# Where gT and w_out_r lie in SBUF: padded weight rows and three activation buffers at different byte offsets

## The chip, the core and the metric

The kernel runs on one core of a Trainium2 chip. A core has TensorE (matmuls, with a separate weight load before each), VectorE (DVE), ScalarE (ACT), GpSimd (POOL) and SyncE (SP, which only issues transfers here). Each engine takes its instructions strictly in order, and semaphores tie the engines to each other and to DMA transfers. Engines work on SBUF, whose tiles have 128 partitions and a byte address within the partition; matmuls write PSUM. The metric is the device time of one execution in microseconds; the median of several executions is compared.

## The reference

The input x has 8 sequences of 3008 positions with 256 channels. The first half is a spectral layer: a real FFT along the sequence, a complex 256x256 linear map with a bias, a soft threshold on real and imaginary parts, and the inverse FFT. The second half is a feed-forward layer on all 24064 positions: 256 to 2048, an ELU, and 2048 back to 256.

```python
X = np.fft.rfft(x, axis=1)
Yr = Xr @ w_r - Xi @ w_i + b_r          # and Yi alike
Yr = np.sign(Yr) * np.maximum(np.abs(Yr) - 0.01, 0.0)
y = np.fft.irfft(Yr + 1j * Yi, n=3008, axis=1)
h = y @ w_in
g = np.where(h > 0.0, h, np.exp(np.minimum(h, 0.0)) - 1.0)
out = g @ w_out                          # float32, 24064 x 256
```

## The kernel before

**The spectral layer.** 3008 = 47 x 64, and the FFT is done as matmuls in stages called units: A (`unit_A`, L129), X, M (the linear map), B and Y. Between A and X, and between B and Y, the data goes through DRAM, to come back with other rows on the partitions: A tiles are written to a DRAM tile DA (L157) and read back as Z (`load_Z`, L159); B tiles go to DB and come back as Bs (`load_Bs`, L267). Unit Y writes yT, the layer's output with channels on partitions, in bf16.

**The feed-forward layer.** The 24064 positions are cut into 47 blocks of 512, the 2048 hidden features into 8 pairs of 128-wide strips. One iteration i of the main loop (L844) is one block and one pair, so there are 376 iterations, 47 to a sequence. In an iteration:

- `front` (L705) computes hps, the hidden values of 2 strips for 512 positions, with four bf16 matmuls of 512 columns (L715). ACT then computes Et from it: exp (L729, or L724 in halves), or a relu and an exp (L726, L727).
- `elu` (L746) has DVE (L754) or POOL (L752) clamp Et.
- `finish_elu` (L734), called in the next iteration, has DVE combine hps and Et into gT (L740 or L742): 128 partitions by 2 strips by 512 positions in float32r, 4096 bytes per partition. This is also what frees hps in PSUM, of which there are two buffers in ordinary iterations, so `front` of two iterations later waits for it.
- `back` (L757), two iterations later (LAG = 2), multiplies gT by w_out_r: eight matmuls L773, each with a 128x128 slice of gT as weights and one 256-column row of w_out_r as the moving operand, both float32r, adding up in PSUM over the eight pairs. After the last pair the sums are copied to osb and sent to the output.

The units of the next sequences are spread over the iterations of the current one by `plan` (L800); each iteration carries at most a few of them ahead of its L715, in TensorE's order. The order of every engine is thus written out by the program; nothing is rearranged at run time.

**The tiles.** w_out_r (L64) is one SBUF tile of 16 rows of 256 float32r values per partition: row ft starts 1024 x ft bytes after the tile's start, and the tile's start is a multiple of 64 bytes. It is filled by two transfers from POOL's queue (`load_w_out`, L581). gT has a pool tag of its own with three buffers in `late3` (L566, L736), which lie 4096 bytes apart, all starting at a multiple of 64 bytes. The same three buffers serve once more: in the opening, unit A of the second sequence runs ahead (L663), and its second and third chunk (L133) take two of them, buffers 0 and 2 by address, until L157's transfers to DRAM have read them. In the built program the first gT of the main loop takes the remaining buffer, the second gT takes that same buffer again, and from the third on the buffers rotate. A gT that reuses a buffer waits for what read it last: an L773 group, or a transfer of A.

Of the kernel before, what the change touches and what calls it, by code (L numbers as in the profile page):

```python
# [10 lines left out]
BF16 = mybir.dt.bfloat16  # L11
F32 = mybir.dt.float32
F32R = mybir.dt.float32r
# [16 lines left out]
def kernel(  # L30
# [12 lines left out]
    P = nc.NUM_PARTITIONS  # L43

    B, S, D = x.shape
    assert D == 256 and S == N1 * N2
    DFF = moe_w_in.shape[1]
    E = moe_w_out.shape[1]
    assert E == 256 and DFF % (2 * P) == 0
    NFT = DFF // P  # L50
# [5 lines left out]
    constp = ctx.enter_context(tc.tile_pool(name="constp", bufs=1))  # L56
# [4 lines left out]
    wcat_r = constp.tile([P, 2, 2 * D], BF16, name="wcat_r")  # L61
    wcat_s = constp.tile([P, 2, 2 * D], BF16, name="wcat_s")
    w_in_s = constp.tile([P, 2, DFF], BF16, name="w_in_s")
    w_out_r = constp.tile([P, NFT, E], F32R, name="w_out_r")  # L64
    bias_bc = constp.tile([P, 2 * D], F32, name="bias_bc")
    bias_p = constp.tile([P, 2 * D], BF16, name="bias_p")
    lam_n = constp.tile([P, 1], F32, name="lam_n")
# [22 lines left out]
    TB = 512  # L90
# [4 lines left out]
    n = B * PER  # L95
# [3 lines left out]
    A_of = {}  # L99
# [18 lines left out]
    def unit_ps(name, alone):  # L118
        if alone:
            return pre2.tile([P, 2, 512], F32, name=name, tag="pre2")  # L120
        return psF.tile([P, 2, 512], F32, name=name, tag="fps")

    def evac(dst, src, on_dve):
        if on_dve:
            nc.vector.tensor_copy(dst, src)  # L125
        else:
            nc.scalar.copy(dst, src)  # L127

    def unit_A(b, u, alone=False, on_dve=False, ahead=False):  # L129
        ci, uu = u // 2, u % 2  # L130
        if uu == 0:
            if ahead and ci > 0:
                A_of[b, ci] = late3.tile([P, 8, D], BF16, name="A", tag="gT")  # L133
            elif alone:
                A_of[b, ci] = wk4.tile([P, 8, D], BF16, name="A", tag="Bs")
            else:
                A_of[b, ci] = wk2.tile([P, 8, D], BF16, name="A", tag="A")
            if ci == 0:
                DA_of[b] = dram.tile([NJ, P, D], BF16, name="DA", tag="DA")
        xt, A = xts[ci], A_of[b, ci]  # L140
        dav = DA_of[b].rearrange("j p d -> p j d")
        ps = unit_ps("aps", alone or ahead)
        for j in range(2):
            nc.tensor.matmul(  # L144
                ps[:, j, :], lhsT=M1[:],
                rhs=xt[:, 4 * uu + 2 * j : 4 * uu + 2 * j + 2, :], start=True, stop=True,
            )
        evac(
            A[:, 4 * uu : 4 * uu + 4, :].rearrange("p n d -> p (n d)"),
            ps[:].rearrange("p a b -> p (a b)"), on_dve,  # L150
        )
        j0 = 8 * ci
        if alone:
            j0 += 4 * uu
            nc.sync.dma_start(dav[:, j0 : j0 + 4, :], A[:, 4 * uu : 4 * uu + 4, :])
        elif uu == 1:
            nc.sync.dma_start(dav[:, j0 : j0 + 8, :], A[:])  # L157
# [155 lines left out]
    with tc.tile_pool(name="stagep", bufs=1) as stagep:  # L313
# [186 lines left out]
        def fA(u):  # L500
            unit_A(0, u, alone=True)
            if u < 5:
                idle_pe(3)
# [60 lines left out]
    gatep = ctx.enter_context(tc.tile_pool(name="gatep", bufs=2))  # L564
    late2 = ctx.enter_context(tc.tile_pool(name="late2", bufs=2))
    late3 = ctx.enter_context(tc.tile_pool(name="late3", bufs=3))  # L566

    w_in_v = moe_w_in.rearrange("(c p) f -> p c f", p=P)
    w_out_v = moe_w_out.rearrange("(t p) e -> p t e", p=P).bitcast(F32R)
# [93 lines left out]
    for u in range(6):  # L663
        unit_A(1, u, on_dve=bool(u % 2), ahead=True)
        if u == 1:
            scale_w_in(1, True)
            for w in (2, 3):
                load_Bs(0, w)
            gate(Bs_of[0, 2][:, 0, 0:1])
            load_w_out(1)  # L670
            load_w_in(3)
        idle_pe(2)
# [60 lines left out]

    def finish_elu():  # L734
        for i, hps, Et, whole, halves in late_elu:
            gT = late3.tile([P, 2, TB], F32R, name="gT", tag="gT")  # L736
            for s in range(2) if halves else (slice(0, 2),):
                o, h, e = gT[:, s], hps[:, s], Et[:, s]
                if whole:
                    nc.vector.scalar_tensor_tensor(o, e, -1.0, h, ALU.add, ALU.max)  # L740
                else:
                    nc.vector.scalar_tensor_tensor(o, h, 0.0, e, ALU.max, ALU.add)  # L742
            g_of[i] = gT
        late_elu.clear()
# [52 lines left out]
    def put(kind, b, *a):  # L797
        return ({"A": unit_A, "X": unit_X, "M": unit_M, "B": unit_B, "Y": unit_Y}[kind], (b, *a))
# [45 lines left out]
    for i in range(n + LAG):  # L844
        if i < n:
            r = i % PER
            if r == 0:
                f0, f1 = plan(i // PER)
                used = [bool(u0 or u1) for u0, u1 in zip(f0, f1)]
            free = not used[r]  # L850
            bare = bare + 1 if free else 0
            calm = free and (i >= n - 2 or (r + 2 < PER and not used[r + 1] and not used[r + 2]))
            for f, a in f0[r]:
                f(*a)
            on_act = any(f is unit_M for f, a in f0[r])
            h = front(i, calm and bare % 3 == 1, on_act, free and i > 0)
        finish_elu()
        if i < n:
            for f, a in f1[r]:
                f(*a)  # L860
            split = i > LAG and (i - LAG) % NPAIR == NPAIR - 1
            if split:
                back(i - LAG, True)
            elu(i, *h, free and i > 0, on_act)
        else:
            split = False
        if i >= LAG and not split:
            back(i - LAG, False)
# [30 lines left out]
```

## Time and profile before

| what | value |
|---|---|
| median of 3 executions | 911.94 us (911.36 to 913.53) |
| profiled execution | 911.36 us, of which span 909.6 us |
| granted TensorE clock, mean | 0.997 |
| L773, 3008 matmuls | busy 477.0 us |
| L715, 1728 matmuls | busy 389.9 us |
| DVE's gT (L740, L742), 470 instructions | 222.8 and 242.2 us |
| ACT's exp L729, 198 instructions | busy 204.0 us |

The profile's page gives busy times and shares for each engine; PE is TensorE's matmuls and PEld its weight loads, which overlap them. Matmuls are pipelined, and the end of one is modelled, so durations of neighbours overlap: what a matmul costs in a stream is the distance from its start to the next start. The chain of work that ended last follows, from the end backwards, at each step what released the step; a row gives start, length and what it was, and "x8" that eight instructions in a row are merged. In the table of waits a row gives who waited for whom, the total in us, how often, and the longest. A group's row gives line, engine, operation, tiles, shape and count, then busy time and the mean ns of one, then the idle time before them and who ended it.

### The profile page before, as it was taken

How to read it: one execution, taken by the hardware profiler on the slowest of the kernel's cores; microseconds unless marked ns; L12 is line 12 of the kernel's file. 1: busy time of each engine (PE TensorE's matmuls, PEld its weight loads, DVE VectorE, ACT ScalarE, POOL GpSimd, SP SyncE). 2: the span in 40 equal slices, each digit the busy share in tenths (PEclk: the TensorE clock that was granted, in tenths of full speed). 3: DMA queues.
4: the chain of work that ended last, by engine and by line, in shares of the span. 5: the costliest groups of instructions: out<-in, count | busy, mean ns of one | idle time of the engine just before them, and what ended most of it. 6: DMA issues, size and time to landing. Idle time of an engine off the chain costs nothing.

```text
span 909.6 us, 17270 instructions
## 1 busy us (share of the span) xinstructions
PE 893.2 (98%) x6721; PEld 652.3 (72%) x6721; DVE 717.5 (79%) x891; ACT 696.8 (77%) x850; POOL 314.9 (35%) x438
## 2 busy tenths in 40 slices
PE   8989999999999999999999999999999999999997
PEld 3447667876688667886678766787667866777775
DVE  8669778887788778897788877888778877778776
ACT  6768788777878778787787888778887877767664
POOL 6701540333321441405404153033332134443664
PEclk9999999999999999999999999999999999999999
DMA  8997116721283215732166032752228111231011
GB/s 270 309 269 228 47 48 186 209 70 47 77 241 124 71 47 143 190 109 85 56 201 194 24 99 59 217 161 72 69 72 230 30 42 47 82 82 48 24 48 46
DMA packets 90670, 106.24 MB, mean 117 GB/s; under 512 B 5270, under 2 KB 81308, under 8 KB 87228
## 3 DMA queue, kind: packets, MB, share of 16 engines
q1 hardware_dynamic: 84332, 77.62, 30.6%
q0 software_dynamic: 5968, 27.26, 9.1%
q8 instruction: 52, 0.85, 0.4%
q10 hardware_dynamic: 288, 0.26, 0.1%
q14 instruction: 30, 0.25, 0.1%
HBM read 55.32 MB, written 49.81 MB: 116 GB/s over the span
## 4 chain that ended last, share of the span: by engine, by line
PE 85%; DVE 5%; ACT 3%; DMA 3%; issue 2%; POOL 1%; SPq 1%; DVEq 0%; ACTq 0%; POOLq 0%
PE ps_o L773 34%; PE hps L715 34%; PE mps L192 9%; PE yps L282 2%; PE bps L244 2%; PE xps L175 2%; PE aps L144 2%; DMA Bs<-DB 2%; DVE gT L742 1%; DVE Et L754 1%; ACT Et L729 1%; ACT Et L726 1%; DMA xt<-in_x_dram 1%; DVE osb L784 1%; ACT Bz L257 1%
## 5 line engine op out<-in xcount | busy, mean ns | idle before, releaser
L773 PE MATMUL ps_o<-w_out_r,gT 128*128 128x256 f32 x3008 | 477.0, 301 | 0.2 <-DVE gT L740 0.2
L773 PEld LDWEIGHTS ps_o<-w_out_r,gT 128*128 128x128 f32 x3008 | 403.4, 189 | 50.3 <-DVE osb L784 1.3
L715 PE MATMUL hps<-yT,w_in_s 128*128 128x512 bf16 (+4 forms) x1728 | 389.9, 353 | 2.5 <-DVE gT L742 1.2
L740 DVE SCALAR_TENSOR_TENSOR gT<-Et,hps 128x512 fp32r<-128x512 f32 (+1 forms) x272 | 222.8, 848 | 75.3 <-POOL Et L752 38.2
L742 DVE SCALAR_TENSOR_TENSOR gT<-hps,Et 128x1024 fp32r<-128x1024 f32 x198 | 242.2, 1223 | 16.5 <-PE ps_o L773 1.0
L715 PEld LDWEIGHTS <-w_in_s 128*128 128x128 bf16 x1728 | 141.6, 98 | 129.4 <-issue 23.0
L729 ACT ACTIVATE Et<-hps 128x1024 f32<-128x1024 f32 x198 | 204.0, 1030 | 13.2 <-PE hps L715 6.7
L752 POOL TENSOR_SCALAR Et<-Et 128x512 f32<-128x512 f32 x187 | 111.4, 615 | 222.9 <-ACT Et L724 222.9
L754 DVE TENSOR_SCALAR Et<-Et 128x1024 f32<-128x1024 f32 x198 | 137.0, 692 | 48.0 <-ACT Et L729 40.1
L210 POOL TENSOR_SCALAR clip<-yb 128x512 f32<-128x512 f32 x84 | 51.7, 615 | 316.0 <-DVE yb L202 278.6
L724 ACT ACTIVATE Et<-hps 128x512 f32<-128x512 f32 x188 | 102.1, 595 | 63.9 <-PE hps L715 63.9
L726 ACT ACTIVATE Et<-hps 128x1024 f32<-128x1024 f32 x84 | 86.3, 1027 | 71.5 <-PE hps L715 71.0
L211 POOL TENSOR_TENSOR Y<-yb,clip 128x512 bf16<-128x512 f32 x84 | 107.2, 1276 | 7.0
L727 ACT ACTIVATE Et<-Et 128x1024 f32<-128x1024 f32 x84 | 88.8, 1058 | 2.7
L202 DVE TENSOR_TENSOR yb<-mps,bias_bc 128x512 f32<-128x512 f32 x89 | 61.4, 689 | 35.4 <-PE mps L192 28.6
L127 ACT CAST XT<-xps 128x768 bf16<-128x768 f32 x61 | 48.8, 800 | 15.8 <-PE xps L175 15.8
L127 ACT CAST yT<-yps 128x752 bf16<-128x752 f32 x63 | 49.7, 788 | 14.2 <-PE yps L282 14.1
L192 PE MATMUL mps<-wcat_r,XT 128*128 128x512 bf16 x192 | 58.2, 384 | 0.8 <-ACT Bz L257 0.3
L127 ACT CAST A<-aps 128x1024 bf16<-128x1024 f32 x45 | 45.6, 1014 | 15.3 <-PE aps L144 13.8
L192 PE MATMUL mps<-wcat_s,XT 128*128 128x512 bf16 x192 | 57.1, 379 | 0.0
L192 PEld LDWEIGHTS <-XT 128*128 128x128 bf16 x384 | 30.8, 98 | 29.6 <-DVE XT L125 0.6
L257 ACT CAST Bz<-bps 128x1024 bf16<-128x1024 f32 x46 | 46.0, 1000 | 2.5 <-PE bps L244 2.5
(110 smaller groups left out, 412.9 us busy)
## 6 DMA issues: line engine op xcount, KB each, us to landing
xt<-in_x_dram POOLq DMA_DIRECT2D x21, 1024.0 KB, 7.1
out_dram<-osb SPq DMA_DIRECT2D x158, 128.0 KB
Bs<-DB SPq DMA_DIRECT2D x32, 384.0 KB
DA<-A SPq DMA_DIRECT2D x21, 512.0 KB
DB<-Bz SPq DMA_DIRECT2D x21, 512.0 KB
Z<-DA SPq DMA_DIRECT2D x7, 1152.0 KB
Z<-DA SPq DMA_DIRECT2D x11, 384.0 KB
xt<-in_x_dram POOLq DMA_DIRECT2D x6, 512.0 KB, 5.9
```

Source lines behind the costliest of these rows:

```text
L127: nc.scalar.copy(dst, src)
L192: nc.tensor.matmul(ps, lhsT=XT[:, dt, c, o : o + P], rhs=wm[:, dt, :], start=(not biased and m == 0 and dt == 0), stop=(m == 1 and dt == 1),)
L211: nc.gpsimd.tensor_tensor(Y_of[b, q][:, i, :], yb, clip[:], ALU.subtract)
L715: nc.tensor.matmul(hps[:, s, c0:c1], lhsT=w_in_s[:, dt, ft * P : ft * P + P], rhs=yT_of[b][:, dt, t0 : t0 + c1 - c0], start=(dt == 0), sto ...
L724: nc.scalar.activation(E_[:, s], hps[:, s], AF.Exp)
L726: nc.scalar.activation(E_, hps[:], AF.Relu, scale=-1.0)
L729: nc.scalar.activation(E_, hps[:], AF.Exp)
L740: nc.vector.scalar_tensor_tensor(o, e, -1.0, h, ALU.add, ALU.max)
L742: nc.vector.scalar_tensor_tensor(o, h, 0.0, e, ALU.max, ALU.add)
L752: eng.tensor_scalar(E_[:, s], E_[:, s], 1.0, 0.0, ALU.min, ALU.max)
L754: nc.vector.tensor_scalar(E_, E_, 1.0, -1.0, ALU.min, ALU.add)
L773: nc.tensor.matmul(po[q][:, i_ % 2, :], lhsT=gT[:, s, i_ * P : i_ * P + P], rhs=w_out_r[:, ft, :], start=(ft == 0 and i_ % 2 == 0), stop=( ...
```

## The change

The rows of w_out_r become 272 values apart, 1088 bytes, of which 256 are used; so row ft starts 64 x ft bytes further than before relative to a multiple of 1024. The three gT buffers become three tiles of their own in a pool `late1`, 4160 bytes each, and within them the 4096 bytes used start 0, 32 and 16 bytes in. The tiles' starts are multiples of 64. Iteration i takes buffer (i + 2) mod 3; A's second and third chunk take buffers 0 and 1. So the first gT takes buffer 2, the second buffer 0 and the third buffer 1. All tiles that come after w_out_r in SBUF move up by 1024 bytes or a little more, and keep their offset from a multiple of 64. The instructions of each engine and their order stay the same.

```diff
-    w_out_r = constp.tile([P, NFT, E], F32R, name="w_out_r")
+    w_out_p = constp.tile([P, NFT, E + 16], F32R, name="w_out_r")
+    w_out_r = w_out_p[:, :, 0:E]
@@ unit_A
-                A_of[b, ci] = late3.tile([P, 8, D], BF16, name="A", tag="gT")
+                A_of[b, ci] = shifted(ci - 1, 8 * D, BF16, "A").rearrange("p (n d) -> p n d", d=D)
@@ after the pools
+    late1 = ctx.enter_context(tc.tile_pool(name="late1", bufs=1))
+    SHIFT = (0, 32, 16)
+
+    def shifted(k, n_, dt, name):
+
+        k %= 3
+        o = SHIFT[k] * n_ // (8 * TB)
+        w_ = n_ + 64 * n_ // (8 * TB)
+        t = late1.tile([P, w_], dt, name=name, tag=f"gT{k}")
+        return t[:, o : o + n_]
@@ finish_elu
-            gT = late3.tile([P, 2, TB], F32R, name="gT", tag="gT")
+            gT = shifted(i + 2, 2 * TB, F32R, "gT").rearrange("p (s t) -> p s t", s=2)
```

## The prediction

> **What bounds the kernel now.** I read the page first: engine totals, the chain of work that ended last, the costliest groups.
>
> ```profile
> span 909.6 us, 17270 instructions
> PE 893.2 (98%) x6721; PEld 652.3 (72%) x6721; DVE 717.5 (79%) x891; ACT 696.8 (77%) x850; POOL 314.9 (35%) x438
> ...
> PE 85%; DVE 5%; ACT 3%; DMA 3%; issue 2%; POOL 1%; SPq 1%; DVEq 0%; ACTq 0%; POOLq 0%
> ...
> L773 PE MATMUL ps_o<-w_out_r,gT 128*128 128x256 f32 x3008 | 477.0, 301 | 0.2 <-DVE gT L740 0.2
> L773 PEld LDWEIGHTS ps_o<-w_out_r,gT 128*128 128x128 f32 x3008 | 403.4, 189 | 50.3 <-DVE osb L784 1.3
> ```
>
> TensorE bounds it, and L773, which reads both tiles that the change moves, is the largest single item (with L715 a third of the chain each). So a few ns on each of 3008 matmuls would show. Then the chain in order of time, in a steady stretch around 460 us:
>
> ```profile
> 453.80 0.86 PE hps L715 x4
> 454.67 0.94 PE ps_o L773 x8
> 455.61 0.54 PE bps L244 x8
> 456.15 0.97 PE hps L715 x4
> 457.12 0.94 PE ps_o L773 x8
> 458.06 0.47 PE aps L144 x2
> 458.53 0.88 PE hps L715 x4
> 459.41 0.92 PE ps_o L773 x8
> ```
>
> No other engine stands between the pieces: what TensorE saves or loses here reaches the end. The eight matmuls of L773 take 0.92 or 0.94 us: 115 or 117.5 ns each. Start to start in the trace, the six inner ones of a group average 116.1 ns. There are two patterns: 119, 118, 113, 114, 113, 113 (mean 115.0), and about 118 throughout (117.75). Last, the chain around 60 us, with the waits of DVE and of SP's queue:
>
> ```profile
> 59.98 1.24 DVE gT L742
> 61.22 0.04 issue
> 61.26 1.02 PE hps L715 x4
> 62.28 0.95 PE ps_o L773 x8
> 63.23 0.02 issue
> 63.25 1.24 DVE gT L742
> 64.49 0.04 issue
> 64.53 1.02 PE hps L715 x4
> ```
> ```profile
> DVE gT L742 <- PE ps_o L773: 1.0, 1, 1.0
> ```
> ```profile
> SPq L164 <- DMA DA<-A: 9.3, 1, 9.3
> ```
>
> The second gT (63.25) waited 1.0 us for the L773 group that still read its buffer, because it shares it with the first. The other two buffers hold the last two chunks of A, whose transfers to DRAM are slow: SP, which needs both, waits 9.3 us for them.
>
> **Part 1: the order in which the buffers are taken.** In the changed program every engine issues the same instructions in the same order as before; only waits differ. The second gT now takes buffer 0 and waits for the transfer of A's first late chunk, the third takes buffer 1 and waits for the last chunk. No L773 group is waited for there any more. The trace's semaphore records give the landings: 64.10 us (issued 55.70) and 66.64 us (issued 56.27). I follow it with the durations of the timeline:
>
> - Second gT: its Et is ready at 62.2, the landing comes at 64.10, so it starts near 64.15 in place of 63.25: 0.9 us later. Behind it in DVE's order stand L754 and the third gT. L715 of the fourth iteration, which needs the PSUM pair that this gT reads, moves from 64.53 to 65.43.
> - Third gT: DVE could start it at 65.43 + 0.69 (L754) = 66.0 and a little; the second landing at 66.64 holds it to 66.69, in place of 65.11: 1.58 later, ending at 67.92.
> - L715 of the fifth iteration waits for that: 67.96 in place of 66.67.
> - DVE now has L658 (0.42), L754 (0.69) and gT (1.23), 2.34 us, in each of the next two iterations, against 2.15 us of TensorE; so DVE leads there. The fourth gT starts at 69.05 (was 67.44), the fifth at 71.41 (was 69.70). The seventh L715 follows the fifth gT: 72.68 in place of 70.98, 1.70 later.
> - After that DVE needs 1.92 us an iteration and TensorE 2.15, and the 1.7 us stay. Z and A's loads do not move, but nothing on the chain after 66 us waits for them: the waits there (Bs from DRAM at 149 us, the osb copies) hang on TensorE's own progress.
>
> So +1.7 us. Ends: if the landings came before 62.2, the old 1.0 us wait goes and nothing takes its place: -1.0. If they came 1 us later (nearest row: the spread of w_out_r's two landings is far larger, 9.6 to 14.4 us after issue), +2.7. I keep +1.7 because the six transfers ahead of them are unchanged and the DMA engines are nearly full there.
>
> **Part 2: the addresses in the steady loop.** Two thirds of the gT reads and writes now start 32 or 16 bytes past a multiple of 64, and w_out_r's rows step through 64-byte multiples in place of all lying alike modulo 1024. No row shows TensorE reading at such an offset.
>
> - Writes of gT by DVE: 198 x 1223 + 84 x 1215 + 188 x 684 ns, 473 us of work, two thirds of it at an offset. The nearest row: ACT's copies into yT alternate between a start at a multiple of 64 bytes and 32 past it (slices of 1504 bytes), and both take 786 ns. So I put this at 0. It has cover of about 0.2 us an iteration (1.92 against 2.15); gone, DVE would lead.
> - Reads by TensorE, down: all groups in the short pattern would save 8 x 1.1 x 376 = 3.3 us, every spacing at 113.3 ns 2.8 x 3008 = 8.4 us. The floor is L715's own 256-column pieces, 109.6 ns in the trace: 6.5 x 3008 = 19.6 us.
> - Reads by TensorE, up: all groups in the long pattern: 1.65 x 3008 = 5.0 us. The farthest row is a bf16 matmul just after the stream switches between types, 226 ns in place of 216: 10 x 2005 offset matmuls = 20 us.
> - I take 0. The 113 and 118 ns patterns occur at one and the same set of offsets: iterations 5 to 9 of nearly every batch open with the same two or three long spacings, though buffer and w_out_r rows differ each time; elsewhere they alternate from batch to batch. That is what a dependence on the surrounding work looks like, rather than one on the address.
>
> The Trainium skill, "SBUF — State Buffer", section "Who interferes with whom", holds that only DVE and GpSimd share a port pair and that TensorE waits for nobody; by that rule addresses against other engines' accesses are worth nothing, and the sum stays at part 1. The same page's lines of 16 bytes also speak against a gain: 0, 16, 32 and 1088 are whole lines. The trace agrees only in part, since it does show TensorE losing about 5 ns a matmul in some surroundings.
>
> - Extra columns of w_out_r: no instruction reads them. Its two loads still move 1024 KB each in 1 KB rows; the second, issued at 59.87, has until 71.6 before L773 first reads it and took 9.6 us. 0, hidden by that margin of 2 us.
> - A in the second buffer starts 32 bytes in: one transfer of 512 KB, in part 1's ends.
>
> Sum on the profiled execution (911.36 us with 909.6 of span): 911.36 + 1.7 = 913.1. That execution lies 0.58 below the median 911.94, so the forecast is 913.6.
>
> **The rivals.**
>
> - *Faster, 0.29.* The spacing is a conflict of the weight read (gT) with the moving read (w_out_r) or with DVE's write of the next gT, and spreading the addresses removes it. For: the spacing exceeds that of bf16 by 6.5 ns with no wait in view, and L773 is the one matmul with two float32r streams. Against: the patterns follow the surroundings. Price -3.3 to -8.4, at most -19.6, plus 1.7: 910.3 to 905.2, at most 894. It decides once over 1.5 ns a matmul goes.
> - *Slower, 0.32.* A read that starts off a multiple of 64 bytes costs a little at its head or locks into the long pattern. Weight loads of L773 take 188 ns against 98 for bf16 and follow each other at the pace of the matmuls, so no slack is seen. For: nothing before reads off such a multiple, so the price is open. Against: ACT's writes. Price +5.0 to +20 plus 1.7: 918.6 to 933.6. With part 1 there, half a nanosecond on each of the 2005 is enough to pass 0.3%.
> - *The change does nothing, or part 1 turns into its gain,* because the transfers of A land earlier: 910.9 to 911.9. It is within the class of the forecast.
>
> **How the numbers follow.** About 0.3% (2.7 us) is what a measurement of this kernel can tell from no change. The forecast case, part 1 alone with its ends (910.9 to 914.6), has 0.39, counted as no change with the third rival. Faster 0.29, slower 0.32. The range reaches to the all-113 case, 905, and past the all-long-pattern case to 920; I leave about 0.07 below and 0.12 above.
>
> **What would show it.** Part 1: the second gT waits for the DMA of A to about 64.1, the third to about 66.6, L715 then follows 1.7 us later than before, and the wait for L773 is gone. Part 2: the L773 pieces of the chain remain at 0.92 to 0.94 us and DVE's gT at 1223 ns. Pieces near 0.91 throughout mean the first rival; 0.95 and more, or two of three iterations longer than the third, the second. The prediction is wrong if the spacing of L773 moves by over a nanosecond.

## The result and the profile after

The changed kernel takes 918.59 us (median of 6, 918.0 to 920.65) against 912.66 us (median of 6): a ratio of 1.0072, 95% interval 1.0059 to 1.0085. That is 6.6 us slower (5.4 to 7.8). The forecast was 913.6 us; the time lies inside the stated range of 905 to 920, but at the price of the slower rival, not in the case that I held likeliest. The granted TensorE clock is 0.997 in both profiled executions, so it plays no part.

From the page of the changed kernel (all line numbers after the new function are 11 higher: L784 was L773, L726 was L715, L753 was L742, L765 was L754):

```profile
span 916.2 us, 17270 instructions
PE 898.2 (98%) x6721; PEld 655.8 (72%) x6721; DVE 718.1 (78%) x891; ACT 696.8 (76%) x850; POOL 313.4 (34%) x438
...
PE 88%; DMA 3%; ACT 3%; DVE 3%; issue 1%; SPq 1%; POOL 0%; ACTq 0%; DVEq 0%; POOLq 0%
...
L784 PE MATMUL ps_o<-w_out_r,gT 128*128 128x256 f32 x3008 | 482.5, 303 | 0.1
L784 PEld LDWEIGHTS ps_o<-w_out_r,gT 128*128 128x128 f32 x3008 | 406.8, 189 | 50.0 <-DVE osb L795 1.0
...
L753 DVE SCALAR_TENSOR_TENSOR gT<-hps,Et 128x1024 fp32r<-128x1024 f32 x198 | 242.1, 1223 | 18.0 <-DMA DA<-A 2.6
```

TensorE bounds the kernel more than before (88% of the chain, was 85%). Its busy time grew by 5.0 us, and the group that reads the moved tiles by 5.5 (482.5, was 477.0), so that group is all of it. DVE's gT costs 1223 ns as before: writing 16 or 32 bytes past a multiple of 64 costs nothing that shows. DVE now waits 2.6 us for the transfers of A.

The chain of the changed kernel in the same steady stretch as shown before:

```profile
453.30 0.94 PE ps_o L784 x8
454.24 0.88 PE mps L193 x4
455.12 0.86 PE hps L726 x4
455.98 0.94 PE ps_o L784 x8
...
463.40 0.94 PE ps_o L784 x8
464.34 0.54 PE bps L245 x8
464.88 0.97 PE hps L726 x4
465.85 0.95 PE ps_o L784 x8
466.80 0.46 PE aps L145 x2
467.26 0.88 PE hps L726 x4
468.13 0.95 PE ps_o L784 x8
```

The pieces of 0.92 us are gone from this stretch; the eight matmuls take 0.94 or 0.95 us (0.93 once, at 461.12), while the neighbours (0.86 to 0.97, 0.54, 0.46) are what they were to 0.01 us. Start to start, the six inner matmuls of a group average 118.01 ns, before 116.12. And the opening, in the chain and in the table of DVE's and of TensorE's waits:

```profile
56.35 8.84 DMA DA<-A
65.32 1.24 DVE gT L753
66.59 1.02 PE hps L726 x4
67.62 0.94 PE ps_o L784 x8
68.56 0.35 PE yps L283 x8
68.91 1.00 PE hps L726 x4
```
```profile
DVE gT L753 <- DMA DA<-A: 2.6, 2, 2.1
```
```profile
PE hps L726 <- DVE gT L753: 2.5, 2, 1.8
```

TensorE's row before the change:

```profile
PE hps L715 <- DVE gT L742: 1.2, 2, 1.0
```

The second gT starts at 65.32, just behind the landing of A's chunk (65.19), and TensorE stands 1.8 us for it, where its longest such wait was 1.0. The chain now enters the loop through that transfer.

Where the 6.6 us by which the span grew lie, by the start of the L773 groups in the two traces: 1.2 us are there before the first group (61.93, now 63.16), 1.3 us come up to the ninth group, 3.9 us from there to the last group, 0.3 us after it. In the 3.9 us the inner spacings account for 4.0, the first and last matmul of the groups for 0.9, and the rest of the stretch is 1.0 shorter; what shortens there I did not follow. The first 1.2 us is scatter and not the change's doing: a run below with the same addresses reaches its first group at 61.95, and one with the same offsets and the same order at 62.01.

### The profile page after: what moved, and what is told of

It is laid out like the page before. It is cut to its first block, busy times and chain, and to the rows that moved or that the text cites. A ratio compares the mean times of both kernels' runs of the same rounds, so it can differ in the third digit from the quotient of the medians.

```text
span 916.2 us, 17270 instructions
## 1 busy us (share of the span) xinstructions
PE 898.2 (98%) x6721; PEld 655.8 (72%) x6721; DVE 718.1 (78%) x891; ACT 696.8 (76%) x850; POOL 313.4 (34%) x438
## 4 chain that ended last, share of the span: by engine, by line
PE 88%; DMA 3%; ACT 3%; DVE 3%; issue 1%; SPq 1%; POOL 0%; ACTq 0%; DVEq 0%; POOLq 0%
PE ps_o L784 36%; PE hps L726 34%; PE mps L193 9%; PE xps L176 2%; PE yps L283 2%; PE bps L245 2%; PE aps L145 2%; DMA Bs<-DB 1%; DMA DA<-A 1%; ACT Et L737 1%; ACT Bz L258 1%; SPq L802 0%; DMA xt<-in_x_dram 0%; DVE gT L751 0%; DMA DB<-Bz 0%
## 5 line engine op out<-in xcount | busy, mean ns | idle before, releaser
L784 PE MATMUL ps_o<-w_out_r,gT 128*128 128x256 f32 x3008 | 482.5, 303 | 0.1
L784 PEld LDWEIGHTS ps_o<-w_out_r,gT 128*128 128x128 f32 x3008 | 406.8, 189 | 50.0 <-DVE osb L795 1.0
L726 PE MATMUL hps<-yT,w_in_s 128*128 128x512 bf16 (+4 forms) x1728 | 390.0, 353 | 3.3 <-DVE gT L753 2.5
L753 DVE SCALAR_TENSOR_TENSOR gT<-hps,Et 128x1024 fp32r<-128x1024 f32 x198 | 242.1, 1223 | 18.0 <-DMA DA<-A 2.6
L726 PEld LDWEIGHTS <-w_in_s 128*128 128x128 bf16 x1728 | 141.7, 98 | 130.9 <-issue 23.5
L765 DVE TENSOR_SCALAR Et<-Et 128x1024 f32<-128x1024 f32 x198 | 137.0, 692 | 49.5 <-ACT Et L740 42.2
```

Of the source, the lines that this page charges most:

```text
L726: nc.tensor.matmul(hps[:, s, c0:c1], lhsT=w_in_s[:, dt, ft * P : ft * P + P], rhs=yT_of[b][:, dt, t0 : t0 + c1 - c0], start=(dt == 0), sto ...
L765: nc.vector.tensor_scalar(E_, E_, 1.0, -1.0, ALU.min, ALU.add)
L784: nc.tensor.matmul(po[q][:, i_ % 2, :], lhsT=gT[:, s, i_ * P : i_ * P + P], rhs=w_out_r[:, ft, :], start=(ft == 0 and i_ % 2 == 0), stop=( ...
```

## The experiments

The theories. The order of the buffers costs the opening some 1.7 us (my working). For L773: theory O, a weight read off a multiple of 64 bytes costs; theory P, the pitch of the rows does; theory D, the place of gT against w_out_r counts; theory B, what counts is that the buffer read and the one DVE writes lie differently. "Spacing" is always the mean distance of starts of the six inner matmuls of an L773 group, from the trace; 116.12 ns before. The few distances over 140 ns are left out. Each value is of one profiled execution; where several programs place both tiles alike, their values agree within 0.03 ns (116.12, 116.15 and 116.15; 118.01 and 118.04). The ratio of times holds more than the spacing: in the profiled executions of the pitch of 1088, of w_out_r by 192 and of the pitch of 1152, all three in the old order, a gT waited 1.0 to 2.0 us for A as well.

**The parts alone.** The pitch alone:

```diff
-    w_out_r = constp.tile([P, NFT, E], F32R, name="w_out_r")
+    w_out_p = constp.tile([P, NFT, E + 16], F32R, name="w_out_r")
+    w_out_r = w_out_p[:, :, 0:E]
```

> The kernel before with rows of w_out_r 1088 bytes apart; the gT buffers stay in their pool and all start at a multiple of 64 bytes. If the offsets of gT are what lengthens L773 (theory O: weights read 16 or 32 bytes off a multiple of 64), the inner spacing of L773 stays at 116.1 ns and the time at 912 to 913 us. If the pitch of the rows does it (theory P), the spacing goes to about 118 ns and the time up by 5 to 6 us, to about 918. In neither does the second gT wait for A's transfer, since the buffers are taken as before.

Measured: spacing 118.12 ns, ratio 1.0044 (1.0031 to 1.0056), 916.5 us. Theory P is met and theory O falls as the only cause: every gT still starts at a multiple of 64. The spacing shows the address directly: groups of an even pair of strips run at 119.1 ns, of an odd pair at 117.2, so it repeats with every second step of 128 bytes; before they differ by some 0.3 ns. The time rose by 4.0 us (2.8 to 5.1), less than the 5 to 6 that I expected. One thing more I had expected otherwise: the fourth gT did wait for A, whose last chunk landed only at 69.6 us.

Own tiles, pitch and offsets as before:

```diff
-    w_out_p = constp.tile([P, NFT, E + 16], F32R, name="w_out_r")
+    w_out_p = constp.tile([P, NFT, E], F32R, name="w_out_r")
-    SHIFT = (0, 32, 16)
+    SHIFT = (0, 0, 0)
```

> The changed kernel without padding of w_out_r and with all three offsets at 0: only the order in which buffers are taken is left. My working of this part gives +1.7 us (the second gT starts with A's landing, 0.9 us late, the third 1.6 us late) with L773 at its old spacing of 116.1 ns: about 914 us. If the order costs nothing: 912.5, and L715 waits no longer than before.

Measured: 1.0043 (1.003 to 1.0056), 917.1 us, spacing 117.31 ns. It was not the clean run of the order that I meant it to be. The tiles are 4160 bytes long, so buffer 1 starts 64 bytes further against a multiple of 128 than the other two, and its groups run at 119.05 ns; buffers 0 and 2 at 116.4 and 116.5. The next runs follow from that accident.

The offsets alone:

```diff
-    w_out_p = constp.tile([P, NFT, E + 16], F32R, name="w_out_r")
+    w_out_p = constp.tile([P, NFT, E], F32R, name="w_out_r")
```

> The changed kernel without padding of w_out_r; gT at 0, 32 and 16 bytes. Theory O: L773 spacing about 118 ns and all of the loss, about 918.5 us, with groups that read buffers 1 and 2 longer than those of buffer 0. Theory P: spacing 116.1 ns, only the order of the buffers is left, about 914 us. If both parts act on the distance between weight rows and moving rows, each alone could cost part of it.

Measured: 1.0065 (1.0046 to 1.0084), 918.1 us, spacing 117.90 ns: buffer 0 116.4, buffer 1 119.6, buffer 2 117.7. The two buffers off a multiple of 64 are the longer ones, as theory O has it. By the spacing each part alone costs what both do (118.12 and 117.90 against 118.01), so they do not add.

The changed kernel with buffers taken in the old order:

```diff
-            gT = shifted(i + 2, 2 * TB, F32R, "gT").rearrange("p (s t) -> p s t", s=2)
+            gT = shifted(2 if i == 0 else i + 1, 2 * TB, F32R, "gT").rearrange("p (s t) -> p s t", s=2)
```

> The changed kernel, but the second gT takes buffer 2 again, as before the change, and the third and fourth take 0 and 1; addresses and offsets as in the changed kernel. The waits for A's transfer go and the second gT waits 1 us for L773 instead. If the order of the buffers costs 1.7 us, this runs 1.7 us faster than the changed kernel, about 917; the spacing of L773 stays at 118 ns. If the order costs nothing it stays at 918.6.

Measured: 1.0038 (1.0026 to 1.0051), 916.0 us, spacing 118.04 ns. The wait for A is gone from DVE's table; the second gT waits for L773 (here L784) again:

```profile
DVE gT L753 <- PE ps_o L784: 1.4, 1, 1.4
```

With the wait go 2.6 us by the medians (3.1 by the ratios); 3.5 us (2.4 to 4.7) stay, which is the price of the addresses.

**What about the addresses.** Four runs in the old order, rows 1024 bytes apart, all three buffers alike. For the first, third and fourth, against the changed kernel with the old order:

```diff
-    w_out_p = constp.tile([P, NFT, E + 16], F32R, name="w_out_r")
-    w_out_r = w_out_p[:, :, 0:E]
+    w_out_r = constp.tile([P, NFT, E], F32R, name="w_out_r")
-    SHIFT = (0, 32, 16)
+    SHIFT = (64, 64, 64)        # or 32, or 16
-        w_ = n_ + 64 * n_ // (8 * TB)
+        w_ = n_ + 256 * n_ // (8 * TB)
```

and for the second, with SHIFT at 0:

```diff
-    w_out_r = constp.tile([P, NFT, E], F32R, name="w_out_r")
+    w_out_p = constp.tile([P, NFT * E + 64], F32R, name="w_out_r")
+    w_out_r = w_out_p[:, 48 : 48 + NFT * E].rearrange("p (t e) -> p t e", e=E)
```

> Rows of w_out_r 1024 bytes apart, buffers of gT taken in the old order, all three moved alike by 64 bytes: gT at 192 past a multiple of 256, w_out_r at 64. In the run with own tiles and no offset, buffer 1 lies at 192 by the tile's odd size and its groups run at 119.05 ns against 116.4 of the other two. Theory D (the distance between the weight read and the moving read of the same matmuls counts): all groups run at about 119 ns, some 8 us lost in the sum over 3008 matmuls, of which 5 to 6 show as time (917 to 918). Theory B (what counts is that the buffer read and the buffer that DVE writes lie differently): three buffers alike again run at 116.1 ns, 912.4 us.

Measured: spacing 119.05 ns (119.0, 119.2, 119.0 by buffer), 1.0065 (1.005 to 1.008), 918.6 us. This is the longest spacing of all, with everything at a multiple of 64 and the three buffers alike. Theories O and B fall as the only cause. The buffers lie 4352 bytes (17 x 256) apart, so two of them differ by 256 modulo 512, and yet they agree: a move of gT by 256 bytes does not show. Its chain:

```profile
453.34 0.94 PE ps_o L783 x8
...
458.71 0.95 PE ps_o L783 x8
```

> As the kernel before, buffers taken in the old order, gT at 128 past a multiple of 256 as before, but the whole of w_out_r moved by 192 bytes, rows still 1024 apart: w_out_r at 0 past a multiple of 256. The distance from gT to w_out_r is then that of the run with gT moved by 64. Theory D: same spacing as in that run, about 119 ns. Theory B: 116.1 ns and 912.4 us, since gT and everything that DVE and ACT touch lie as before.

Measured: spacing 118.26 ns, 1.0043 (1.0028 to 1.0058), 916.5 us. Moving only w_out_r costs as well, with gT and what DVE and ACT write where they were modulo 256. So the places of both tiles count. Theory D is not shown by that: the same distance modulo 256 gave 119.05 in the run before it and 118.26 here, so the distance is not all, and no run moves both tiles alike, which would keep the distance and change both places.

> Rows 1024 bytes apart, old order, all three gT buffers moved by 32 bytes (160 past a multiple of 256, off a multiple of 64). Theory O (a start off a multiple of 64 bytes itself costs): every group at 119 ns or more, 918 us. Theory D: the spacing takes another value, of either sign, and is the same for all three buffers. Theory B: 116.1 ns.

Measured: spacing 117.91 ns (117.9 to 118.0 by buffer), 1.0038 (1.0023 to 1.0053), 916.1 us.

> The same with 16 bytes (144 past a multiple of 256). Theory O: about 118 to 119 ns in every group, as with 32. Theory D: a value of its own; buffer 2 of the run with offsets alone, which lay 16 past a multiple of 256 with w_out_r at 64, had 117.7 ns. Theory B: 116.1 ns. If a value is near 113.3 ns, the lower end of the spacing before, this is a faster kernel than before, by up to 8 us.

Measured: spacing 118.65 ns (118.6 to 118.8 by buffer), 1.0062 (1.0045 to 1.0078), 917.9 us. With 16, 32 and 64 bytes the buffers agree with each other and each distance has a value of its own, as theory D expects; a dependence on gT's own place would look the same. Theory O misses its size with 32 bytes (119 ns or more expected). No value is near 113.

**Does it repeat?** All buffers moved by 128 bytes (SHIFT at 128 in the diff above):

> Rows 1024 bytes apart, old order, all three gT buffers moved alike by 128 bytes, so that they start at a multiple of 256. If the distance between gT and w_out_r counts modulo 128 bytes, 64 being the good one, the spacing of L773 is 116.1 to 116.5 ns as before (buffer 2 of the run with own tiles and no offset lay like this and had 116.5) and the time 912.4 us, while moves by 16, 32 and 64 cost 3.5 to 6 us. If any move away from the old place costs, whatever its size, the spacing is about 118 ns and the time 916 to 918 us.

Measured: spacing 116.73 ns, 1.0012 (1.0003 to 1.0022), 912.7 us. A move by 128 brings the spacing back to within 0.6 ns of the old one, where 64 was the worst: the size of the move does not matter, its place within 128 bytes mostly does.

Rows 1152 bytes apart, 128 more than before, instead of 64:

```diff
-    w_out_r = constp.tile([P, NFT, E], F32R, name="w_out_r")
+    w_out_p = constp.tile([P, NFT, E + 32], F32R, name="w_out_r")
+    w_out_r = w_out_p[:, :, 0:E]
```

> The kernel before with rows of w_out_r 1152 bytes apart (1024 + 128), nothing else. If the distance counts modulo 128, every row stands 64 from gT as before: 116.1 to 116.5 ns, 912.4 us, against 118.1 ns and 916.5 us of 1088 bytes (1024 + 64), where every other row stands at 0. If an uneven pitch itself costs, or the distance counts modulo 256 or more, the spacing is 117 to 119 ns in the groups whose rows lie 128 further, and the time 914 to 917 us.

Measured: spacing 118.14 ns, 1.0053 (1.0039 to 1.0066), 916.6 us, no better than a pitch of 1088. My expectation of a plain period of 128 falls here. The matmuls on rows at 64 past a multiple of 256 lie to gT just as in the kernel before, where these same matmuls take 116.2 ns; here they take 117.5. So what the neighbours read counts too. (Those on rows at 192 take 118.8. That they are longer is no sign of a bad row: with w_out_r moved by 192, where all rows lie alike, the same two halves of a group take 117.6 and 118.9. Whether 192 is good when all rows lie there, no run shows; the run with 128 has only its distance.) From pair to pair the rows step by 256 bytes, and the eight pairs agree within 0.3 ns.

The traces hold one thing more that no theory above explains. Unit A's matmuls (L144: float32r too, M1 as weights, xt as moving operand, 512 columns) read neither moved tile, and in the four runs that move gT alone by 16, 32, 64 and 128 bytes their own tiles lie at the very addresses of the kernel before. Where one of their pairs stands behind a group of L773, the distance within the pair averages 228.7 ns in the kernel before (228.4 and 228.5 in the other two runs with the old places), but 231.1, 228.3, 229.6 and 233.8 in those four; the commonest distance is 226 before and 235 with gT by 128, where L773 itself runs nearly as before. The bf16 matmuls of unit M stay at 218.7 to 218.9 in all runs. So the spacing of a float32r matmul depends also on the places of tiles that it does not read. Whether it carries over from the matmuls ahead of it or comes from other engines' reads and writes of gT at the time, no run separates, and the mechanism stays open.

**The order alone, at the old addresses,** from the run with own tiles:

```diff
-        w_ = n_ + 64 * n_ // (8 * TB)
+        w_ = n_
```

> The order in which the changed kernel takes the gT buffers, alone: own tiles of 4096 bytes without offset, so that every address is the old one; rows 1024 bytes apart. L773 keeps 116.1 ns. My working gives +1.7 us from the two waits for A's transfer, with landings as late as 69.6 us seen in other runs up to +3: 914 to 915.5. The difference between the changed kernel and its run with the old order was 2.6 us. If the order is not the cause, 912.4.

Measured: spacing 116.15 ns, 1.0027 (1.0014 to 1.004), 914.8 us: 2.5 us (1.3 to 3.6) for the order of the buffers and nothing else. Its chain in the opening, and the row of DVE's waits:

```profile
56.29 12.11 DMA DA<-A
68.40 0.03 issue
68.43 0.05 DVEq L753
68.48 0.04 issue
68.52 1.24 DVE gT L753
69.76 0.04 issue
69.80 1.02 PE hps L726 x4
```
```profile
DVE gT L753 <- DMA DA<-A: 4.5, 2, 2.8
```

Here A's last chunk landed at 68.4, and the third gT started right behind it.

**A version without either wait,** the kernel before with A's last chunk in a buffer of osb:

```diff
-                A_of[b, ci] = late3.tile([P, 8, D], BF16, name="A", tag="gT")
+                pool, tag = (late3, "gT") if ci == 1 else (late2, "osb")
+                A_of[b, ci] = pool.tile([P, 8, D], BF16, name="A", tag=tag)
```

> The kernel before, with all addresses of gT and w_out_r as they were, but A's last chunk of the opening in a buffer of osb, which is not used before 79 us, in place of a gT buffer. Two gT buffers are then free from the start: the second gT waits neither for L773 nor for A's last transfer, the third waits for A's first transfer at most. If the waits for gT buffers in the opening are worth what I say, the 1.0 us wait of the second gT goes, and the time falls by about 1 us to 911.4; if the opening has slack, nothing changes.

Measured: 0.9996 (0.9985 to 1.0006), 911.5 us: no difference that can be told, though the interval still holds 1 us. The wait of the second gT is gone. By the start of the groups it is 1.0 us ahead of the kernel before from the second to the fourth group, and 0.5 behind by the ninth. The chain there:

```profile
56.16 12.46 DMA DA<-A
...
69.18 8.30 DMA Z<-DA
77.48 0.04 issue
77.53 0.52 PE xps L176 x8
```

```profile
PE xps L176 <- DMA Z<-DA: 1.5, 4, 0.5
```

Unit X needs Z, and Z is read only after A's last chunk has landed. That chunk landed at 68.62 us here, 2.0 us later than in the kernel before, and Z with it, so part of the lead went into waits for Z (0.9 us of them between 70 and 90 us). Whether the lead would have lasted with an early landing, this one execution does not show. In the run of the order alone the opening lost 3.0 us from the first to the ninth group, of which 0.8 came back by the last. No run was told apart from the kernel before as faster.

All runs, spacing and time against the kernel before:

| run | gT past a multiple of 256 (buffers 0, 1, 2) | w_out_r rows past a multiple of 256 | order | spacing ns | ratio |
|---|---|---|---|---|---|
| before | 128, 128, 128 | 64 | old | 116.12 | 1 |
| the change | 128, 224, 16 | 64, 128, 192, 0 | new | 118.01 | 1.0072 |
| pitch 1088 | 128, 128, 128 | 64, 128, 192, 0 | old | 118.12 | 1.0044 |
| own tiles | 128, 192, 0 | 64 | new | 117.31 | 1.0043 |
| offsets | 128, 224, 16 | 64 | new | 117.90 | 1.0065 |
| the change, old order | 128, 224, 16 | 64, 128, 192, 0 | old | 118.04 | 1.0038 |
| gT by 64 | 192, 192, 192 | 64 | old | 119.05 | 1.0065 |
| w_out_r by 192 | 128, 128, 128 | 0 | old | 118.26 | 1.0043 |
| gT by 32 | 160, 160, 160 | 64 | old | 117.91 | 1.0038 |
| gT by 16 | 144, 144, 144 | 64 | old | 118.65 | 1.0062 |
| gT by 128 | 0, 0, 0 | 64 | old | 116.73 | 1.0012 |
| pitch 1152 | 128, 128, 128 | 64, 192 | old | 118.14 | 1.0053 |
| order alone | 128, 128, 128 | 64 | new | 116.15 | 1.0027 |
| A in osb | 128, 128, 128 | 64 | no wait | 116.15 | 0.9996 |

## Why the prediction was right or wrong

- *What bounds the kernel* was read rightly: a nanosecond or two on each L773 is what moved the time, with no other engine in between.
- *Part 1, the order of the buffers:* the mechanism was right, down to which gT waits for which chunk. The term was sized at +1.7 us and measured 2.5 (1.3 to 3.6) alone; taking the old order in the changed kernel gave 2.6 by the medians. The size hangs on when A's chunks land, and I had one execution: the last chunk landed at 66.64 there, and between 66.4 and 69.6 us in the other runs. My upper end allowed 1 us for that, and the runs showed 3. The end of -1.0 left a step out: in the run with A in osb the old wait went and 1.0 us was won, but it was gone by the ninth group, in an execution where TensorE waited for Z next.
- *Part 2, writes of gT:* 0 was right; 1223 ns before and after.
- *Part 2, reads by TensorE:* "I take 0" is the step that failed. The addresses cost 3.5 us (2.4 to 4.7). My argument was that 113 and 118 ns patterns occur at one and the same set of offsets, so they follow the surroundings. That is true and proves nothing about offsets: in the kernel before, gT and w_out_r lie the same way modulo 256 in every group, so its trace cannot show a dependence on something that never varies. The surroundings matter, and the address matters as well: 116.12 ns became 118.01.
- *The slower rival* named the right consequence with a cause that is not needed. The pitch of 1088 and the move by 64 keep every start on a multiple of 64 bytes, and cost as much or more. Its low price, all groups in the long pattern (117.75 ns), is close to the 118.0 that came. It gave 5.0 us for all 3008; from the ninth group on the trace has 4.9 us in longer spacings, first and last included, of which 1.0 came back elsewhere. That the sum 918.6 is the measured time to 0.1 us is luck: the addresses cost less than 5.0, the order more than 1.7, and the range reached that far for a pattern that I could not explain.
- *The faster rival* had it that all buffers and rows alike is a conflict to be spread out. The kernel before has the shortest spacing of the placements tried, and spreading made it longer. One of its grounds was misread: L773 is not the one matmul with two float32r streams. Unit A's L144 has them as well, and it too runs over its bf16 counterpart of 512 columns, 228.7 ns against 216.
- *The rule weighed in part 2,* from the Trainium skill's page "SBUF — State Buffer", section "Who interferes with whom", would have left part 1 alone, about 914. The runs disagree with the conclusion that was drawn from it: with the same instructions and the same order, a move by 64 bytes changes the spacing of float32r matmuls by 2.9 ns and the time by 0.65%. Whether the rule itself fails, no run shows, since the loss may arise between TensorE's own reads.

## What to carry to other kernels

In this kernel, where float32r matmuls follow each other at 116 ns with a weight load before each, the byte places of the weights and of the moving operand were worth 0.6 to 2.9 ns a matmul. A padded row, a longer tile or a tile added ahead of them moves such places unseen. Compare them before and after an edit that seems only to move memory, and undo a move by padding whole tiles to a multiple of 256 bytes: moves by 256 showed nothing here, neither between gT buffers nor between pairs of rows. And when the trace shows one value of a quantity only, it says nothing about what another value would do: give that term a range of both signs and a price, not zero.

## What the runs showed of the hardware that I had not expected

- The spacing of L773 depends on the place of gT and w_out_r in steps as small as 16 bytes: 116.1 (as before), 118.65 (gT by 16), 117.9 (by 32), 119.05 (by 64), 116.7 (by 128). Between the kernels before and after, the first spacing of a group lengthened as the inner six did, by 1.9 ns on average.
- Matmuls whose own two tiles lie as before run longer when their neighbours' rows lie elsewhere (pitch 1152: 117.5 ns against 116.2), and unit A's float32r matmuls change by up to 5 ns when only gT moves, which they do not read. That leaves the mechanism open; neither the distance alone nor a period of 128 bytes alone explains all runs.
- The landing of one 512 KB transfer in the crowded opening varies by 3 us from run to run (66.4 to 69.6 us), and with the new order the kernel waits for it.
